# Two head pairs' k and v by the hardware queue in fp32, larger tile bursts, and a new order of pieces, in a fused linear-attention and channel-mix kernel

## The chip, the cores and the metric

One core of a Trainium2 chip runs the whole program. Its engines each work through their own list of instructions in order: TensorE (PE in the profile; PEld is its weight load), VectorE (DVE), ScalarE (ACT), GpSimd (POOL, which here only issues loads) and SyncE (SP, which here only issues transfers). They meet through semaphores. The metric is the device time of one execution in microseconds, median of several runs.

## The reference

What has to be computed, cut to its core (B = 8 batches, H = 8 heads, S = 576 positions, D = 64, so C = H * D = 512; F = 1024):

```python
kv  = einsum('bhsd,bhse->bhde', k, v)
o   = einsum('bhsd,bhde->bhse', q, kv)
o   = o / sqrt(mean(o * o, -1) + 1e-6) * g_norm
x   = o.transpose(0, 2, 1, 3).reshape(B, S, C)
x_prev = x shifted by one position, zeros first
xk  = mu_k * x + (1 - mu_k) * x_prev ;  xr likewise with mu_r
k2  = maximum(xk @ w_k, 0) ;  out = sigmoid(xr @ w_r) * ((k2 * k2) @ w_v)
```

All inputs and the output are fp32 in DRAM.

## The kernel before

The work is cut into named pieces. A piece is a Python function that records a few instructions on one engine; `plan.emit` (L60 on) goes through the string `ORDER` word by word and records the pieces in that order, so each engine's list of instructions is the order of its words. A word `name@D` or `name@A` says on which of VectorE and ScalarE a piece runs that could run on either. Nothing is reordered later: an engine whose next piece waits stands still, whatever is ready behind it.

Attention of batch b, in two halves z = 0, 1 of four heads each:

- `ld.q`, `ld.k`, `ld.v` (L251) load a tensor through GpSimd's software queue, which converts fp32 to bf16 on the way. Batches 0 and 1 load by z, 288 KB each as bf16; later batches load whole, 576 KB. The weights (`ld.wk0`, `ld.wk1`, `ld.wr`, `ld.wv0`, `ld.wv1`, L266, 512 KB each) use the same queue. At most eight of its transfers are under way: the ninth issue waits until the first has landed. Loads also wait until one of three buffers of their tensor is free.
- `kv` (L286) makes the 64 x 64 products of k and v, `q` (L294) transposes q, `u` (L301) multiplies the two. All three use quarters of TensorE's array (64 x 64 tiles); the rest of TensorE's work uses the whole array, except `ss` of batches 2 and up. Their results stand in two PSUM buffers, `at`. `kc`, `qc` and `uc` copy them to SBUF (L172 on ScalarE, L174 on VectorE), and `sq` squares u. `u`, `uc` and `sq` come in two column parts each: `u3.01` is batch 3, z = 0, part 1.
- `ss` sums squares per head. In batches 2 and up one `ss` serves all heads (L409), `rs` takes the reciprocal root (L306, tile `rsc`), and `sp.z` (L455), on SyncE, copies its rows to all partitions by four transfers for each z. `mul.z` (L423, VectorE) multiplies into `xT`.
- `wr.z` copies 63 columns inside `xT`, `d` subtracts neighbours, `mk` and `mr` scale the difference, `xk` and `xr` (L331) add: the inputs of the channel mix.

The channel mix, in nine groups g of 512 rows that straddle the batches: `k` (L518 for g = 0, L542) with `relu` (L503) and `ksq` (L552); `r` (L564) with `sig` (L574); `v` (L584) with `out` (L597), which multiplies by `sig`; `st` (L493), on SyncE, stores 128 rows by two transfers. `mm`, two PSUM buffers, holds the results of k, r and v in turn, and `out` has three SBUF buffers, each free again when both of its stores have landed. `g.wk`, `g.wr` scale the weights by g_norm. `z:512` (L482) is a matmul of zeros that adds nothing; it only keeps TensorE working.

Of the kernel before, what the change touches and what calls it, by code (L numbers as in the profile page):

```python
# [7 lines left out]
FP32 = mybir.dt.float32  # L8
# [7 lines left out]
ld.q0.0 seta small setb ld.k0.0 ld.v0.0 ld.q0.1 ld.v0.1 ld.k0.1 ident ld.wk0 id9 ld.q1.0 z:512 z:512 z:512 z:512  # L16
z:512 z:512 z:512 z:512 z:512 z:512 z:512 q0.01 ld.wk1 tr9 qc0.01@A cols z:512 q0.00 qc0.00@A ld.v1.1 z:512 z:512
z:512 z:512 z:512 z:512 z:512 z:512 kv0.0 ld.v1.0 kc0.0@A z:512 u0.01 u0.00 uc0.01@D uc0.00@A ld.k1.1 sq0.01@D
sq0.00@D z:512 z:512 z:512 z:512 z:512 ss0.01 ss0.00 rs0.01 ld.k1.0 rs0.00 mul0.01 z:512 z:512 q0.11 qc0.11@D ld.wr
mul0.00 z:512 kv0.1 q0.10 d0.0a kc0.1@A qc0.10@D mk0.0a@A z:512 u0.11 uc0.11@D u0.10 wr0.0@A sq0.10@A d0.0w sq0.11@D  # L20
uc0.10@A g.wk00@D ld.q1.1 z:512 z:512 z:512 z:512 ss0.10 xk0.0a d0.0b ss0.11 rs0.10 k0.000 ld.wv0 rs0.11 mul0.10
q1.0 g.wk01@A d0.1a mk0.1a@D mk0.0b@A xk0.1a mr0.0a@D table k0.001 g.wk10@D ld.wv1 g.wk11@D k0.010 mul0.11 relu0.00
d0.1b ld.q2.01 xk0.0b k0.011 mk0.0w@D mk0.1b@D k0.100 wr0.1@D relu0.01 xk0.1b ld.v2.01 d0.1w ksq0.00 k0.101 mr0.0b@A
mr0.1a@D k0.110 ld.k2.01 relu0.10 xr0.0b ksq0.01 mr0.1b@A xk0.0w ksq0.10 ld.v3.01 kv1 qc1.0@D kc1@A xr0.1b mr0.0w@A
xr0.0a u1.01 u1.00 uc1.01@A k0.111 uc1.00@A g.wr1@D ld.k3.01 g.wr0@D relu0.11 sq1.01@D r0.2 sq1.00@D ld.q3.01
# [5 lines left out]
sq2.00@A xr1.1 relu1.3 k1.5 ksq1.3 ss2 kv3 ksq1.1 rs2 q3.0 ld.k5.01 sp2.0 r1.0 kc3@A relu1.2 qc3.0@D r1.1 ksq1.0
u3.01 q3.1 uc3.01@D sp2.1 r1.2 ld.q6.01 sq3.01@D ld.v5.01 r1.3 sig1.0 qc3.1@D ld.v6.01 ksq1.2 u3.00 u3.10 v1.0.0
uc3.00@D uc3.10@A st0.0 sq3.10@A sq3.00@D v1.0.1 sig1.1 mul2.0 u3.11 q4.1 wr2.0@D d2.0 v1.1.0 mk2.0@A v1.1.1 mul2.1
v1.3.0 qc4.1@A out1.0 v1.2.0 wr2.1@A xk2.0 uc3.11@A st1.0 v1.2.1 sq3.11@A d2.1 v1.3.1 st0.3 mk2.1@D xk2.1 ss3 kv4
out1.1 q4.0 k2.2 ld.q7.01 qc4.0@D rs3 ld.v7.01 k2.3 kc4@D sp3.0 mr2.1@D u4.11 u4.00 uc4.11@D k2.4 uc4.00@A relu2.1
sq4.11@D k2.5 sq4.00@D sp3.1 mr2.0@D u4.01 relu2.2 u4.10 uc4.01@D k2.0 sq4.10@A sq4.01@D k2.1 ksq2.1 uc4.10@A st1.1
xr2.0 ss4 relu2.0 q5.1 xr2.1 k2.6 ksq2.0 k2.7 mul3.0 qc5.1@D r2.0 relu2.3 r2.1 wr3.0@A ksq2.3 rs4 r2.2 ksq2.2 sp4.0
d3.0 r2.3 sig2.0 mk3.0@D q6.1 mul3.1 kv5 sig2.1 q5.0 qc6.1@D st1.3 v2.3.0 kc5@A qc5.0@D v2.1.0 st0.2 wr3.1@D d3.1
u5.11 u5.01 sp4.1 uc5.11@A v2.2.0 mk3.1@D uc5.01@A xk3.1 v2.3.1 mr3.1@D v2.2.1 sq5.01@D st1.2 sq5.11@D v2.0.0 xk3.0
out2.1 u5.10 kv6 uc5.10@A q6.0 ld.k7.01 mul4.0 v2.0.1 st2.2 qc6.0@A mr3.0@D v2.1.1 kc6@A sq5.10@D st2.3 xr3.1 k3.2  # L40
out2.0 u6.10 u5.00 k3.3 uc5.00@A mul4.1 st2.0 k3.4 xr3.0 relu3.1 wr4.1@D k3.5 d4.1 uc6.10@A r3.0 mr4.1@D relu3.2
sq5.00@D r3.1 sq6.10@D wr4.0@D ksq3.1 u6.01 sig3.0 ss5 uc6.01@D k3.0 d4.0 k3.1 sq6.01@D mk4.1@D rs5 kv7 mr4.0@D
relu3.0 q7.0 sp5.1 xr4.0 u6.00 k3.6 kc7@A ksq3.2 qc7.0@A k3.7 mk4.0@D ksq3.0 r3.2 relu3.3 sp5.0 uc6.00@D r3.3
sq6.00@D xk4.0 u6.11 q7.1 uc6.11@D v3.1.0 st2.1 ksq3.3 v3.0.0 sig3.1 mul5.1 v3.1.1 qc7.1@A sq6.11@D xk4.1 ss6 xr4.1
v3.0.1 r4.0 out3.0 r4.1 rs6 st3.0 u7.10 u7.11 sq7.10@A v3.2.0 uc7.11@A st3.1 uc7.10@D v3.3.0 sq7.11@D wr5.1@D sp6.0
# [12 lines left out]
out7.1 r8.3 ksq8.2 st7.2 r8.0 sig8.1 r8.1 st7.3 v8.2.00 sig8.0 v8.2.10 v8.1.10 out8.20 v8.0.00 st8.20 out8.10
v8.0.10 st8.10 v8.3.01 out8.00 v8.3.11 v8.3.00 st8.00 out8.31 v8.3.10 st8.31 out8.30 st8.30
# [40 lines left out]
def kernel(  # L100
# [13 lines left out]
    nc = tc.nc  # L114
# [538 lines left out]
```

## Time and profile before

| | |
|---|---|
| Median of 3 runs | 209.78 us (208.43 to 209.99) |
| Span of the profiled execution | 206.6 us |
| TensorE busy | 193.2 us (94%), 2172 matmuls |
| VectorE busy | 137.8 us (67%) |
| ScalarE busy | 118.6 us (57%) |
| Software queue (q0) | 16.78 MB, 48.3% of 16 engines' span |
| Hardware queue of SyncE (q1) | 12.46 MB, 24.0% |
| v matmuls, L584 | 272 recorded, 62.6 us busy |
| k matmuls, L542 | 288 recorded, 59.2 us busy |
| r matmuls, L564 | 144 recorded, 34.1 us busy |
| Matmuls of zeros, L482 | 34, 10.9 us busy |

Busy times of TensorE overlap, since matmuls are pipelined: one of 512 columns lasts 379 ns, but in a run of them the next ends 216 ns later (16 in 3.45 us). So the place to read is where TensorE stood idle, and for what. The three parts of the span differ. Until about 39 us TensorE waits for the first batches; then it is busy almost without a gap until its last matmul at 202.8 us; 3.8 us remain for the last product and its store.

### The profile page before, as it was taken

The numbers are of one execution on the slowest core, as the hardware profiler recorded it, in microseconds if no ns is written. First come the engines' busy times: TensorE is split into PE (matmuls) and PEld (weight loads), VectorE is DVE, ScalarE is ACT, GpSimd is POOL, SyncE is SP. The second block draws the span as 40 slices with busy tenths as digits, with TensorE's granted clock in tenths as the row PEclk, the third lists the DMA queues.
The fourth block names the chain that finished last, engine by engine and source line by source line (L and its number), as shares of the span: only waits on it lengthen the run. The fifth ranks groups of instructions, "written<-read, shape, count | busy, mean of one in ns | idle before, by whom it ended". The sixth has DMA issues, their size and how long they took to land.

```text
span 206.6 us, 5133 instructions
## 1 busy us (share of the span) xinstructions
PE 193.2 (94%) x2172; PEld 95.7 (46%) x2172; DVE 137.8 (67%) x273; ACT 118.6 (57%) x151; POOL 26.4 (13%) x40
## 2 busy tenths in 40 slices
PE   7797979999799799799999999999999999999992
PEld 2344844544344444354443585444444444444441
DVE  1059988886585999698997798788733623421332
ACT  2279789867577395636896987716725032531310
POOL 7752532202140400000000000000000000000000
PEclk9999999999999999999999999999999999999999
DMA  4999999999999999999433650346004242604155
GB/s 75 162 207 205 206 208 205 208 216 221 210 238 236 231 252 242 223 264 268 116 91 77 149 122 0 71 94 156 0 0 102 62 93 61 143 0 102 24 133 153
DMA packets 25211, 30.10 MB, mean 146 GB/s; under 512 B 2524, under 2 KB 20708, under 8 KB 25188
## 3 DMA queue, kind: packets, MB, share of 16 engines
q0 software_dynamic: 15408, 16.78, 48.3%
q1 hardware_dynamic: 9380, 12.46, 24.0%
q10 hardware_dynamic: 400, 0.52, 0.7%
q8 instruction: 17, 0.28, 0.5%
q14 instruction: 6, 0.05, 0.1%
HBM read 33.56 MB, written 9.44 MB: 208 GB/s over the span
## 4 chain that ended last, share of the span: by engine, by line
PE 68%; DMA 20%; SPq 3%; ACT 2%; POOL 2%; issue 2%; DVE 1%; ACTq 0%; DVEq 0%; POOLq 0%
PE mm L584 26%; PE mm L542 24%; PE mm L564 12%; DMA w_r<-in_moe_w_r_dram 7%; DMA rs<-rsc 5%; DMA k<-in_k_dram 4%; DMA out_dram<-out 3%; SPq L455 2%; PE at L584 2%; PE at L301 2%; PE at L286 1%; PE at L294 1%; SPq L493 1%; POOL q L251 1%; ACT rsc L306 1%
## 5 line engine op out<-in xcount | busy, mean ns | idle before, releaser
L584 PE MATMUL mm<-w_v,sqk 128*128 128x512 bf16 x272 | 62.6, 379 | 0.0
L542 PE MATMUL mm<-xk,w_k 128*128 128x512 bf16 (+1 forms) x288 | 59.2, 356 | 0.0
L503 ACT ACTIVATE relu<-mm 128x1024 bf16<-128x1024 f32 x36 | 36.8, 1022 | 25.8 <-PE mm L542 23.4
L584 PEld LDWEIGHTS <-sqk 128*128 128x128 bf16 x296 | 28.2, 98 | 32.2 <-issue 1.4
L542 PEld LDWEIGHTS <-w_k 128*128 128x128 bf16 x288 | 27.2, 98 | 26.9 <-issue 1.6
L564 PE MATMUL mm<-w_r,xr 128*128 128x512 bf16 x144 | 34.1, 379 | 0.7 <-DVE w_r L180 0.7
L552 DVE TENSOR_TENSOR sqk<-relu 128x1024 bf16<-128x1024 bf16 x32 | 21.6, 687 | 16.4 <-ACT relu L503 16.4
L597 DVE TENSOR_TENSOR out<-mm,sig 128x1024 f32<-128x1024 f32 x16 | 19.6, 1222 | 18.6 <-PE mm L584 18.6
L574 ACT ACTIVATE sig<-mm 128x1024 bf16<-128x1024 f32 x18 | 18.3, 1024 | 22.5 <-PE mm L564 22.5
L564 PEld LDWEIGHTS <-xr 128*128 128x128 bf16 x144 | 13.7, 98 | 16.6 <-issue 1.0
L180 DVE TENSOR_SCALAR md<-d,cols 128x576 bf16<-128x576 bf16 (+2 forms) x62 | 18.2, 344 | 0.3
L172 ACT CAST uT<-at 128x576 bf16<-128x576 f32 (+1 forms) x18 | 11.4, 645 | 11.4 <-PE at L301 11.3
L423 DVE TENSOR_TENSOR xT<-uT,rs 128x1152 bf16<-128x1152 bf16 (+2 forms) x18 | 12.4, 686 | 4.8 <-DMA rs<-rsc 3.0
L188 ACT ACT_TABLE_LOAD x12 | 15.4, 1283 | 0.2
L174 DVE CAST uT<-at 128x576 bf16<-128x576 f32 (+1 forms) x14 | 10.4, 742 | 7.0 <-PE at L301 5.5
L318 DVE TENSOR_TENSOR d<-xT 128x1152 bf16<-128x1152 bf16 (+2 forms) x20 | 12.7, 634 | 0.8 <-ACT xT L172 0.5
L331 DVE TENSOR_TENSOR xk<-md,xT 128x1152 bf16<-128x1152 bf16 (+2 forms) x20 | 12.7, 633 | 0.6 <-ACT md L178 0.4
L331 DVE TENSOR_TENSOR xr<-md,xT 128x1152 bf16<-128x1152 bf16 (+2 forms) x20 | 12.5, 631 | 0.0
L482 PE MATMUL mm<-zero 128*128 128x512 bf16 x34 | 10.9, 452 | 1.2 <-DVE zero L209 1.2
L172 ACT COPY qT<-at 128x1152 bf16<-128x1152 bf16 (+2 forms) x8 | 8.0, 995 | 6.0 <-PE at L294 6.0
L178 ACT ACTIVATE md<-d,cols 128x256 bf16<-128x256 bf16 (+2 forms) x18 | 9.9, 600 | 1.8 <-DVE d L318 1.8
L174 DVE COPY qT<-at 128x1152 bf16<-128x1152 bf16 (+2 forms) x10 | 6.9, 693 | 4.7 <-ACT kv L172 4.2
(54 smaller groups left out, 139.3 us busy)
## 6 DMA issues: line engine op xcount, KB each, us to landing
out_dram<-out SPq DMA_DIRECT2D x67, 128.0 KB, 2.5
q<-in_q_dram POOLq DMA_DIRECT2D x6, 576.0 KB, 23.0
v<-in_v_dram POOLq DMA_DIRECT2D x6, 576.0 KB, 25.7
k<-in_k_dram POOLq DMA_DIRECT2D x6, 576.0 KB, 22.5
rs<-rsc SPq DMA_DIRECT2D x48, 72.0 KB, 5.0
q<-in_q_dram POOLq DMA_DIRECT2D x4, 288.0 KB, 9.7
k<-in_k_dram POOLq DMA_DIRECT2D x4, 288.0 KB, 11.4
v<-in_v_dram POOLq DMA_DIRECT2D x4, 288.0 KB, 11.0
```

The costliest lines, as they stand in the source:

```text
L172: nc.scalar.copy(out=dst, in_=src)
L174: nc.vector.tensor_copy(out=dst, in_=src)
L180: nc.vector.tensor_scalar(out=dst, in0=src, scalar1=col, scalar2=None, op0=ALU.mult)
L188: nc.scalar.preload_act_table_set(name)
L331: nc.vector.tensor_tensor(out=dst[:, 2 * z:2 * z + 2, r0:r0 + w], in0=md.t[:, :, cs], in1=xT[:, :, prev], op=ALU.add)
L503: nc.scalar.activation(out=get(rt), in_=ps.t, func=AF.Relu)
L542: nc.tensor.matmul(get(ps)[:, fc % 2, a0:a1], w_k_sb[:, cc, 128 * fc:128 * fc + 128], xk[:, cc, x0:x0 + a1 - a0], start=(cc == 0), stop=(c ...
L552: nc.vector.tensor_mul(out=get(sqk)[:, 2 * f2:2 * f2 + 2, :], in0=rt.t, in1=rt.t)
L564: nc.tensor.matmul(get(ps)[:, ci % 2, :], xr[:, cc, n0:n0 + 128], w_r_sb[:, cc, :], start=(cc == 0), stop=(cc == NHP - 1))
L574: nc.scalar.activation(out=get(sg), in_=ps.t, func=AF.Sigmoid)
L584: nc.tensor.matmul(get(ps)[:, bank, cs], sqk.t[:, fc, 128 * ci:128 * ci + 128], w_v_sb[:, fc, cs], start=(fc == 0), stop=(fc == NFC - 1))
L597: dv = add(f"out{g}.{c2}", "D", lambda _, ps=ps, sg=sg, ot=ot: nc.vector.tensor_mul(out=get(ot), in0=ps.t, in1=sg.t), deps=ms + [sg_done], ...
```

## The change

Four edits, and a new `ORDER` that carries them.

1. k and v of batch 0, z = 0 come by SyncE's hardware queue as fp32 (`hl.v0.0`, `hl.k0.0`), into one of the three buffers of their tensor, and are converted by two new copies of 128 x 1152 (`c.v0.0`, `c.k0.0`, both put on VectorE).
2. `kv` and both `q` of a batch become one piece, `kvq`; both column parts of a `u` become one piece (batches 1 and up).
3. Batch 1 has `kvq` by z, and the k pieces of group 1 take two column blocks and one z each, where they took one column block and all heads.
4. `ORDER` is new throughout. It has 22 matmuls of zeros where there were 34; `ld.wk1` is the first load of the software queue; the loads of batches 2 to 5 come batch after batch.

```diff
+    HW = ("k", "v")
...
+    def load_hw(b, n, z):
+        tmp, dst = Buf(n), kvq[(n, b)]
+        m = slice(2 * z, 2 * z + 2)
+
+        def fp32():
+            return get(tmp)[:, :, :].bitcast(FP32).rearrange("p (m a) c -> p m (a c)", m=2)
+
+        def fn(_):
+            view = src[n][b].rearrange("(m e) (p j) d -> (e p) m (j d)", e=2, j=NJ)
+            nc.sync.dma_start(out=fp32(), in_=view[:, m, :])
+
+        p = add(f"hl.{n}{b}.{z}", "S", fn, bufs=[tmp])
+        loaded[(n, b, z)] = add(f"c.{n}{b}.{z}", "DA", lambda eng: copy(eng, get(dst)[:, m, :], fp32()), deps=[p],
+                                bufs=[tmp, dst])
...
+                    if b == 0 and z == 0 and n in HW:
+                        load_hw(b, n, z)
+                    else:
+                        load(b, n, [z])
...
+                def burst(_, zs=zs, pss=pss):
+                    kv_tiles(get(pss[0]), KC, kin.t, vin.t, zs)
+                    for z, ps in zip(zs, pss):
+                        q_tiles(as_bf16(ps), qin.t, z, range(NJ))
...
+            def u_mm(_, i_s, z=z, qT=qT, uss=uss, parts=parts):
+                for i in i_s:
+                    u_tiles(get(uss[i]), kv.t, qT.t, z, *parts[i])
...
+                if g == 1:
+                    deps = (x_ready[0]["k"][2 * x:2 * x + 2] + [x_wrap["k"][x], x_ready[1]["k"][x]]
+                            + [p_wk[(f2 // 2, z)] for z in range(x + 1)] + [m])
+                    args = ([2 * f2, 2 * f2 + 1], [2 * x, 2 * x + 1])
```

The start of the new order, and its stretch from batch 2's `ss` to group 3's first k pieces (lines as they stand, cut at both ends):

```diff
+seta ident table setb hl.v0.0 c.v0.0@D small ld.wk1 ld.q0.0 ld.v0.1 id9 ld.q0.1 ld.k0.1 z:512 z:512 z:512 z:512 z:512
+z:512 z:512 z:512 z:512 z:512 z:512 z:512 z:512 z:512 tr9 hl.k0.0 c.k0.0@D kv0.0 cols kc0.0@D z:512 q0.01 g.wk10@A
+qc0.01@D q0.00 u0.01 qc0.00@A uc0.01@A sq0.01@D u0.00 sq0.00@A z:512 z:512 z:512 ss0.00 uc0.00@A rs0.00 mul0.00 ss0.01
...
+r1.2 ss2 relu1.0 rs2 st0.1 st0.0 sp2.1 ksq1.1 ksq1.2 ksq1.0 r1.0 r1.3 sig1.1 kvq3 r1.1 qc3.1@A qc3.0@D kc3@D mul2.1
+sp2.0 v1.1.0 u3.1 uc3.11@D sq3.11@A wr2.1@D uc3.10@A sq3.10@A v1.0.0 v1.0.1 v1.1.1 d2.1 mul2.0 sig1.0 u3.0 ld.v4.01
+ld.k4.01 ld.q4.01 wr2.0@A v1.2.0 v1.3.0 v1.3.1 out1.0 d2.0 mk2.1@D xk2.1 uc3.01@D sq3.01@A uc3.00@A sq3.00@A ss3 rs3
+v1.2.1 mk2.0@D xk2.0 kvq4 kc4@A qc4.0@A qc4.1@D out1.1 sp3.1 k2.2 k2.3 sp3.0 st1.2 st0.3 st0.2 u4.1 uc4.10@D mul3.1
+mr2.0@D relu2.1 sq4.11@A k2.0 k2.1 k2.6 uc4.11@A sq4.10@A wr3.1@A relu2.0 u4.0 k2.7 uc4.00@A k2.4 k2.5 ld.q5.01
+ld.v5.01 mr2.1@D relu2.3 xr2.1 xr2.0 ksq2.1 uc4.01@D mul3.0 wr3.0@D sq4.01@A sq4.00@A ld.k5.01 relu2.2 r2.2 ss4 rs4
+ksq2.0 sp4.0 sp4.1 st1.0 ksq2.3 r2.3 v2.3.0 sig2.1 ksq2.2 v2.3.1 v2.2.0 v2.2.1 out2.1 st2.3 st1.1 d3.0 d3.1 r2.0 r2.1
+st1.3 ld.v7.01 ld.q7.01 ld.v6.01 mk3.0@A ld.k6.01 ld.q6.01 ld.k7.01 sig2.0 v2.1.0 kvq5 qc5.1@A v2.0.0 v2.0.1 v2.1.1
+mk3.1@D mr3.1@D mul4.0 xk3.0 kc5@D qc5.0@A xk3.1 mul4.1 u5.0 k3.6 k3.7 out2.0 wr4.0@A xr3.1 wr4.1@D mr3.0@D xr3.0
+uc5.00@A uc5.01@A sq5.01@D sq5.00@D st2.2 relu3.3 d4.0 mr4.0@D ksq3.3 k3.0 k3.1 relu3.0 k3.4 u5.1 uc5.11@A k3.5 k3.2
```

More of the change, by code (lines that the diff above doesn't have):

```diff
@@ L15 @@
 ORDER = """
[L16 to L25, printed above, removed]
@@ L31 @@
[L31 to L40, printed above, removed]
@@ L41 @@
[L41 to L45, printed above, removed]
@@ L60 @@
+st8.30 st8.10 out8.00 st8.00 v8.3.01 v8.3.11 out8.31 st8.31
 """
@@ L260 @@
                 for z in range(NZ):
-                    load(b, n, [z])
+                    if b == 0 and z == 0 and n in HW:
+                        load_hw(b, n, z)
+                    else:
+                        load(b, n, [z])
             else:
@@ L368, in attention, with kv_copy @@
         qd, kvcs = {}, []
-        def kv_piece(name, ps, c, zs):
-            m = add("kv" + name, "T", lambda _: kv_tiles(get(ps), c, kin.t, vin.t, zs), bufs=[ps, kin, vin],
-                    deps=[loaded[(n, b, z)] for n in ("k", "v") for z in zs])
+        def kv_copy(name, dep, ps, c, zs):
             ks = slice(HD * zs[0], HD * zs[-1] + HD)
-            return m, add("kc" + name, "DA", lambda eng: copy(eng, get(kv)[:, :, ks], ps.t[:, :, c + ks.start:c + ks.stop]),
-                          deps=[m], bufs=[ps, kv])
@@ L385, in attention, with lds @@
+        def lds(ns, zs):
+            return [loaded[(n, b, z)] for n in ns for z in zs]
         if b == 0:
             for z in range(NZ):
-                _, kc = kv_piece(f"{b}.{z}", Buf("at"), 0, [z])
-                kvcs.append(kc)
+                ps = Buf("at")
+                m = add(f"kv{b}.{z}", "T", lambda _, ps=ps, z=z: kv_tiles(get(ps), 0, kin.t, vin.t, [z]),
+                        bufs=[ps, kin, vin], deps=lds("kv", [z]))
+                kvcs.append(kv_copy(f"{b}.{z}", m, ps, 0, [z]))
```

131 lines of the change are left out of this document (78 added, 53 removed).

## The prediction

> **What bounds it now.** First the page's slices:
>
> ```profile
> PE   7797979999799799799999999999999999999992
> PEclk9999999999999999999999999999999999999999
> DMA  4999999999999999999433650346004242604155
> ```
>
> TensorE has gaps in the first eight slices (39 us) and almost none after; loads fill the DMA engines until about 99 us. TensorE's timeline of the start:
>
> ```profile
> 1.19 4.56 PE L482 MATMUL mm<-zero 128*128 128x512 bf16 x11 [1.19 <-DVE zero L209]
> ...
> 7.31 1.90 PE L482 MATMUL mm<-zero 128*128 128x512 bf16 x8
> 9.95 0.48 PE L286 MATMUL at<-v,k 64*64 64x64 bf16 x36 [0.74 <-DMA v<-in_v_dram]
> ...
> 18.42 1.03 PE L518 MATMUL mm<-xk,w_k 128*128 128x256 bf16 x8
> 20.75 5.49 PE L518 MATMUL mm<-xk,w_k 128*128 128x256 bf16 x48 [0.89 <-DVE xk L331]
> ```
>
> Useful streaming starts at 18.42. Later idle time is short, and three waits hold most of it (windows of 4 us add up to 4.0 between 39 and 203):
>
> ```profile
> 54.39 0.48 PE L294 MATMUL at<-ident,q 64*64 64x64 bf16 x36 [1.20 <-DMA q<-in_q_dram]
> ...
> 68.42 0.83 PE L286 MATMUL at<-v,k 64*64 64x64 bf16 x72 [0.93 <-DMA k<-in_k_dram]
> ...
> 84.16 0.77 PE L286 MATMUL at<-v,k 64*64 64x64 bf16 x72 [1.42 <-ACT sig L574]
> ```
>
> The third is named after ScalarE, but its burst needed v of batch 5, which stands in the software queue behind tensors of batch 6; I count all three as load waits. Then the chain of waits between them:
>
> ```profile
> 52.13 0.39 PE at L409 x8
> ...
> 52.54 0.75 ACT rsc L306
> ...
> 53.31 0.66 SPq L455
> ...
> 58.14 6.66 DMA rs<-rsc
> ...
> 64.92 0.06 DVE xT L423
> ```
>
> From the end of `ss` (52.5) it takes until 64.9 to multiply the second half; the first was multiplied at 61.1 (VectorE's timeline). Eight spreads cost SyncE 5.4 us to issue, and each lands late. The tile view of `rsc` up to 100 us says
>
> ```profile
> DMA to landing us min/median/max: 5.0/6.7/7.0
> ```
>
> and after 100 us, when no load runs,
>
> ```profile
> DMA to landing us min/median/max: 2.0/2.1/2.7
> ```
>
> Stores show the same: median 6.5 until 90 us, 2.4 from 104 on. Whoever stands behind a spread's `mul` waits some 8.5 us from `ss`, or 12.3 for the second half.
>
> **Start.** Before, q landed first and `kv0.0` ran at 9.95. Now v goes out first on SyncE (0.75; its issue costs 0.6 if it is like a store's, more if rows count), then four small loads (0.37 + 3 x 0.25 = 1.1 us), then k, at about 3. No row shows such a load. Lower bound for k's landing: 3 + 2.2 (least row of a store with no loads running) + 1.4, which is what 288 KB take (GpSimd's issues, freed by landings, come at 8.68, 10.10, 11.56) = 6.6. Upper: 3 + 6.9 (worst store under load) + 2 x 1.4, sharing half and half = 12.7. I take 8.5: only about one load stands in the other queue then, so nearer the lower. Its cast on VectorE, which nothing covers: 0.75 (a copy of 1152 bf16 from PSUM) to 1.5 (two casts of 576 fp32, 0.752 each); I take 1.0. By the Trainium skill ("VectorE: DVE Perf Modes", the mode that uses both read ports) an fp32 copy inside SBUF makes two results a cycle, which would be the lower end; no run here shows it. So `kv0.0` at about 9.6 (7.4 to 14.2). `q0.01` needs q, now second in GpSimd's queue behind 512 KB of weights (2.6 us between landings): about 10. From there to the first k piece the old rows give about 8 (before: 8.5 from `kv0.0`), with the weight scaling, which the old start waited for, out of the way: 18.2 against 18.42, **-0.2** (bounds -2 to +4).
>
> Between there and the first burst of batch 2 (39.07) TensorE waited 0.89 + 0.28 + 0.60 + 0.66 = 2.4 us before. w_r is now the tenth transfer of the software queue rather than the fourteenth, which removes the 0.66; batch 1 by halves shortens the others, and the same products stay: **-1** (0 to -1.5). The fillers dropped here were in idle time and give nothing.
>
> **Bursts.** A switch between whole array and tiles costs about 0.1 us each way (a run of four lasts 0.97 on the chain behind a burst, 0.86 elsewhere). But the old order had already put pieces side by side: from batch 2 on it has 23 groups of tile work, the new one 24. Nothing, plus or minus 0.3. SyncE's one new load, the VectorE casts and table loads (12 switches in either) add nothing past the start.
>
> **Load waits.** Batch 5's v and k now precede everything of batches 6 and 7, and batches 3 and 4 are complete earlier. All three waits go: **-3.6** (0 at worst, if others take their place).
>
> **Spread waits.** This is where I expect the loss. The larger bursts need both `at` buffers back, and the copies that free them stand behind `mul` and `wr` on VectorE and ScalarE. Durations are from one start to the next in the old timelines: r, v and k pieces 0.86 (four matmuls) and 0.1 for a switch; `kvq` 0.74 + 0.73 as kv and q took; two parts of `u` 0.37; on VectorE `mul` 0.69 and a copy of 576 0.68; on ScalarE a copy or square 0.57, `wr` 0.25, `relu` 1.0. With t the end of an `ss`:
> - `u3.0`. TensorE between: r 1.83, `kvq3` 1.45, r and v 1.83, `u3.1` 0.47, three v 2.6, so at t + 8.2 it wants `u3.0`, whose second part needs `uc3.11`. That is behind `mul2.1` on VectorE: 8.5 + 0.69 + 0.68 = 9.9. Wait 1.6.
> - `ss3`. At 10.1 plus three v pieces 2.7 = 12.8 it wants `sq3.00`, fourth on ScalarE after `wr2.0`, which needs `mul2.0` (12.3 + 0.69): 13.0 + 0.25 + 3 x 0.57 = 15. Wait 2.2, taken as 1.8 with the wait of `kvq4` on the same copies.
> - `k2.4`. v 0.96, `kvq4` 1.45, two k 1.83, `u4.1`, three k, `u4.0`, one k 4.5: t + 8.8. It needs `relu2.0`, behind `wr3.1`, behind `mul3.1`: 8.5 + 0.69 + 0.25 + 1.0 = 10.4. Wait 1.6.
> - `v2.3`, behind squares that stand behind `mul3.0`: 0.7.
> - `k3.0`. It needs the PSUM that `out2.0` frees, and `out2.0` the buffer whose last store is `st1.1`. SyncE: root at t + 1.2, eight spreads 5.2, `st1.0`, `st2.3`, then `st1.1`'s second transfer at 9.6, landing 5.4 later at 15.0, and `out2.0` 1.2: 16.2. TensorE has 14.2 of work till then. Wait 2.0; 2.5 with the small ones behind.
>
> Sum **+8.2**. Lower bound +1, with every landing at 2.1; upper +11, at 6.7 throughout.
>
> **Sum.** -0.2 - 1 - 3.6 + 8.2 = +3.4. The profiled execution: TensorE's end moves from 202.8 to 206.2, the 3.8 us of tail stay (the last half product and its store are the same), span 210.0. The median lies 3.2 above the span; with the same distance, 213.2.
>
> **Rivals.**
> - *The spreads land in time.* Fewer transfers collide with them, and landings come at some 2 to 3 us while loads run. Then of +8.2 some 1 remains: -3.8, 206.0, faster. It decides below about 4 us from issue to landing: the loss has to fall to the 4.8 of the gains, and a straight line from 8.2 at 5.4 us to 1 at 2.1 is there at 3.8. Against it: 5.0 is the least of 24 rows, and the loads still run to nearly 100 us. 0.17.
> - *The waits overlap.* One slip gives later spreads time, so half of 8.2 stays: -0.7, 209.1. 0.20.
> - *k is held up at the start.* It waits behind the weights as stores do, lands at 12.7, and the first k piece is at 22: +4 more, 217. 0.13.
> - *TensorE's clock falls.* Fillers took 4.56/11 = 0.41 us at first, later 1.90/8 = 0.24, though PEclk shows 9 in both. The 14 first fillers end near 6.6 and the next matmul comes near 9.6, a pause of 3 us where before it was 0.74. If the slow pace returns, the tile work and the first k pieces of 9.6 to 19 lose about 2: 215.2. 0.08. The Trainium skill ("TensorE: Matmul & The Clock Gate", "What's actually happening") has just this: an idle window of about 3.4 us halves the clock. The slow first fillers agree; no run here shows a return.
> - *My forecast*, all terms near their values, 211.5 to 215: 0.42.
>
> **How the numbers follow.** Likeliest: 213.2. Faster by over 1% (below 207.7; about what a measurement can tell) is the first rival, 0.17; within 1% is the second, 0.20; slower is the rest, 0.63. For the range I leave out most of the first rival below and the far end of the late start above: 207.5 to 217.5.
>
> **What would show it.** Right: no wait on a q, k or v load past 40 us; `u3.0`, `ss3`, `k2.4` and `k3.0` idle 1 to 3 us each, released by VectorE or ScalarE, with idle time there behind `rs<-rsc`, and `out2.0` behind a store; spreads still at 5 us or more. Wrong: TensorE without such gaps between 55 and 100 us (then the first rival), or the first k piece far from 18.2. If TensorE's last matmul falls before 202, the sum failed in the spread term.

## The result and the profile after

The changed kernel takes 226.49 us (median of 4 runs, 225.53 to 226.83), the kernel before 209.88 in the same comparison: ratio 1.0806, 95% interval 1.0747 to 1.0866. That is slower, as forecast, but by 16.6 us where 3.4 were forecast, and outside the range of 207.5 to 217.5. The span of the profiled execution is 223.6 us (before: 206.6), TensorE's last matmul ends at 218.7 (202.8). Of the runs further down, e1, e8 and e12 had one execution each that was over 1.5% above their fastest, and the ratios leave it out while the medians hold it.

The page's slices of TensorE, its granted clock and the DMA engines, of the kernel after (5.6 us each):

```profile
PE   7176899999884993999899999999999999999991
PEclk9958999999997699699999999999999999999999
DMA  6999999999999979966502550550027704600274
```

Before, PEclk was 9 throughout. Now it drops in three places: slices 3 and 4, 13 and 14, and 17, each time in or behind a slice in which TensorE is mostly idle (slice 2 with the digit 1, slice 13 with 4, slice 16 with 3). The start first. VectorE's timeline has the cast of k:

```profile
11.45 0.95 DVE L173 CAST k<-k 128x1152 bf16<-128x1152 f32 x1 [6.17 <-DMA k<-in_k_dram]
```

SyncE issued that load at 2.60, so it was under way for 8.8 us; v, issued at 0.74 and alone until 3.5 us, when the software queue's first packets start, had landed at 4.4. TensorE's timeline (start, length, group, and in brackets the idle time ahead of it and what ended it):

```profile
12.45 0.70 PE L303 MATMUL at<-v,k 64*64 64x64 bf16 x36 [3.52 <-DVE k L173]
...
22.77 1.04 PE L559 MATMUL mm<-xk,w_k 128*128 128x256 bf16 x8
```

The first k piece comes 4.35 us later than before (18.42). This varies between executions: in e3, e4 and e6 below, which have the same start, k's cast begins at 9.97 to 10.29 and the first k piece comes at 21.57 to 22.30. The same timeline between 60 and 95 us:

```profile
68.82 0.32 PE L318 MATMUL at<-qT,kv 64*64 64x288 bf16 x4 [2.76 <-ACT sq L367]
...
70.82 5.28 PE L632 MATMUL mm<-w_v,sqk 128*128 128x512 bf16 x12 [0.46 <-ACT sig L622]
...
89.58 3.36 PE L584 MATMUL mm<-xk,w_k 128*128 128x512 bf16 x8 [3.98 <-ACT relu L544]
```

The three load waits at 54, 68 and 84 us are gone; `u3.0` and `k2.4` wait in their place, behind copies, as the forecast said. But look at the lengths too: twelve matmuls at 70.82 take 5.28 us, where twelve at full pace take 2.75. The chain of waits ahead of 89.58 leads back to a spread, and VectorE's multiply behind it:

```profile
81.19 6.20 DMA rs<-rsc
...
87.51 0.77 DVE xT L464
```

The windows view, in stretches of 3.4 us (stretch, its length, then busy us and instructions of TensorE, its weight load, VectorE, ScalarE and GpSimd, the granted clock, DMA share, GB/s):

```profile
65.90:69.30 3.40, 0.48 (x5) 0.22 (x5) 2.29 (x4) 1.18 (x3) 0.00 (x0) 1.00 1.20 230
69.30:72.70 3.40, 2.33 (x9) 0.94 (x9) 2.65 (x4) 1.65 (x4) 0.00 (x0) 0.51 1.21 208
...
86.20:89.60 3.40, 0.02 (x1) 0.02 (x1) 2.05 (x6) 1.30 (x3) 0.00 (x0) 1.00 1.19 246
89.60:93.00 3.40, 3.40 (x9) 1.21 (x9) 3.37 (x7) 2.16 (x4) 0.00 (x0) 0.53 1.15 274
```

A stretch in which TensorE hardly works (0.48, 0.02) is followed by one with a granted clock of 0.51 or 0.53. In the one at 89.6 it is busy all the time, with 9 matmuls; the same view has 22 in the next 3.4 us, at 0.96. Taken finer, the clock is halved from 11.3 to 18.15, from 69.35 to 76.2 and from 89.8 to 93.2 us, and full elsewhere until TensorE's work ends.

So the 15.9 us of TensorE's end are: +4.35 to the first k piece; -1.4 from there to the fourth v piece (42.0, before 39.07); and 176.7 us from there to the end where it was 163.7. Of these +13, idle time is +7.0 (10.9 against 4.0, from windows of 4 us). The remaining 6.0 are longer busy time; the halved clock at 69.35 to 76.2 and 89.8 to 93.2 accounts for about 4.6 of them, since TensorE is busy for 9.1 us there at half speed, and 1.4 stay unexplained.

### The profile page after: what moved, and what is told of

Its sections match the earlier page's. It is cut to its first block, busy times and chain, and to the rows that moved or that the text cites. A ratio compares the mean times of both kernels' runs of the same rounds, so it can differ in the third digit from the quotient of the medians.

```text
span 223.6 us, 5124 instructions
## 1 busy us (share of the span) xinstructions
PE 197.3 (88%) x2160; PEld 96.6 (43%) x2160; DVE 134.1 (60%) x260; ACT 130.0 (58%) x166; POOL 25.0 (11%) x38
## 3 DMA queue, kind: packets, MB, share of 16 engines
q1 hardware_dynamic: 9924, 13.64, 24.6%
## 4 chain that ended last, share of the span: by engine, by line
PE 49%; DMA 5%; DVE 5%; SPq 2%; ACT 2%; issue 1%; DVEq 0%; ACTq 0%
PE mm L584 17%; PE mm L632 17%; PE mm L612 10%; DMA rs<-rsc 4%; SPq L496 2%; DVE out L645 2%; PE at L632 2%; DMA out_dram<-out 1%; DVE d L335 1%; ACT relu L544 1%; PE at L318 1%; DVE sqk L600 1%; PE at L311 1%; DVE xT L464 1%; PE at L303 1%; SPq L534 1%
## 5 line engine op out<-in xcount | busy, mean ns | idle before, releaser
L632 PE MATMUL mm<-w_v,sqk 128*128 128x512 bf16 x272 | 64.5, 390 | 0.5 <-ACT sig L622 0.5
L584 PE MATMUL mm<-xk,w_k 128*128 128x512 bf16 (+1 forms) x288 | 60.4, 362 | 5.0 <-ACT relu L544 4.0
L632 PEld LDWEIGHTS <-sqk 128*128 128x128 bf16 x296 | 29.2, 100 | 35.3 <-issue 4.1
L645 DVE TENSOR_TENSOR out<-mm,sig 128x1024 f32<-128x1024 f32 x16 | 19.6, 1223 | 26.0 <-PE mm L632 11.3
L367 ACT ACTIVATE sq<-at 128x576 bf16<-128x576 f32 (+2 forms) x23 | 14.9, 660 | 15.6 <-DVE uT L173 14.3
L177 ACT ACTIVATE md<-d,cols 128x576 bf16<-128x576 bf16 (+2 forms) x26 | 17.0, 719 | 5.4 <-DVE d L335 5.4
L179 DVE TENSOR_SCALAR md<-d,cols 128x576 bf16<-128x576 bf16 (+2 forms) x54 | 15.0, 337 | 0.2
L173 DVE CAST uT<-at 128x576 bf16<-128x576 f32 (+1 forms) x17 | 12.6, 755 | 1.8 <-PE at L318 1.8
L348 DVE TENSOR_TENSOR xk<-md,xT 128x1152 bf16<-128x1152 bf16 (+2 forms) x20 | 12.6, 634 | 0.2
L318 PE MATMUL at<-qT,kv 64*64 64x288 bf16 (+2 forms) x128 | 8.2, 309 | 4.4 <-ACT sq L367 3.5
L173 DVE COPY qT<-at 128x1152 bf16<-128x1152 bf16 (+1 forms) x9 | 6.4, 716 | 7.1 <-PE at L311 6.9
L171 ACT COPY qT<-at 128x1152 bf16<-128x1152 bf16 (+2 forms) x9 | 8.6, 965 | 3.5 <-PE at L311 2.4
```

Source lines behind the costliest of these rows:

```text
L173: nc.vector.tensor_copy(out=dst, in_=src)
L177: nc.scalar.mul(out=dst, in_=src, mul=col)
L179: nc.vector.tensor_scalar(out=dst, in0=src, scalar1=col, scalar2=None, op0=ALU.mult)
L348: nc.vector.tensor_tensor(out=dst[:, 2 * z:2 * z + 2, r0:r0 + w], in0=md.t[:, :, cs], in1=xT[:, :, prev], op=ALU.add)
L584: nc.tensor.matmul(get(ps)[:, fc % 2, a0:a1], w_k_sb[:, cc, 128 * fc:128 * fc + 128], xk[:, cc, x0:x0 + a1 - a0], start=(cc == 0), stop=(c ...
L632: nc.tensor.matmul(get(ps)[:, bank, cs], sqk.t[:, fc, 128 * ci:128 * ci + 128], w_v_sb[:, fc, cs], start=(fc == 0), stop=(fc == NFC - 1))
```

## The experiments

Each run is compared with the kernel before on the same chip. Where a gain over the changed kernel is given in us, it is the difference of the two ratios times 209.6; with these intervals it is good to 1.5 to 2.1 us.

| Run | Median us | Ratio to before | 95% interval |
|---|---|---|---|
| the changed kernel | 226.49 | 1.0806 | 1.0747 to 1.0866 |
| e1_fill_start | 223.39 | 1.0618 | 1.0537 to 1.0700 |
| e2_loads_first | 224.68 | 1.0705 | 1.0667 to 1.0743 |
| e3_repeat | 224.13 | 1.0676 | 1.0621 to 1.0731 |
| e4_mul_behind | 218.06 | 1.0380 | 1.0331 to 1.0428 |
| e5_soft_start | 224.67 | 1.0741 | 1.0688 to 1.0794 |
| e6_no_late_loads | 218.62 | 1.0439 | 1.0390 to 1.0488 |
| e7_start_order | 221.63 | 1.0587 | 1.0546 to 1.0629 |
| e8_searched | 214.41 | 1.0232 | 1.0170 to 1.0294 |
| e9_before_loads | 208.94 | 0.9973 | 0.9940 to 1.0006 |
| e10_before_searched | 207.83 | 0.9931 | 0.9903 to 0.9959 |
| e11_searched_again | 215.42 | 1.0279 | 1.0217 to 1.0342 |
| e12_refill_shift | 212.43 | 1.0114 | 1.0045 to 1.0183 |
| e13_small_bursts | 205.91 | 0.9823 | 0.9778 to 0.9868 |

### The clock at the start: e1_fill_start

```diff
 z:512 z:512
+z:512 z:512 z:512 z:512 z:512 z:512 z:512 z:512 z:512 z:512 z:512
 tr9 hl.k0.0 c.k0.0@D
+z:512 z:512 z:512 z:512 z:512 z:512 z:512 z:512 z:512 z:512 z:512 z:512 z:512 z:512
 kv0.0 cols
```

> The changed kernel with 11 more fillers ahead of tr9 and 14 more ahead of kv0.0, so that TensorE has work from 6.0 to about 12 us, where it was idle but for tr9; nothing else is moved. Theory A (the halved granted clock from 11.3 to 18.2 us is set by that pause, and it costs time): the granted clock stays at 1.0 through the start, the first k piece comes at 21.3 rather than 22.8, and the time falls by 1 to 2 us. Rival (the start goes at the pace of the landings and of the copies, and the slow clock hides behind them): the clock stays up as well, but the first k piece stays at 22.3 to 22.8 and the time within 0.5 us.

Measured: faster by 3.9 us. The windows view of this run, where the changed kernel has a clock of 0.50 in the same stretch:

```profile
11.30:14.70 3.40, 2.65 (x86) 1.48 (x85) 0.89 (x4) 2.05 (x3) 1.95 (x3) 1.00 1.21 206
```

The first k piece comes at 21.36, 1.4 us earlier. The times alone would not settle it, because e3, e4 and e6, which have the changed kernel's start and its halved clock, reach it at 21.57 to 22.30. But `kv0.0` runs at the same time here and in the changed kernel (12.50 and 12.45), and from it to the first k piece it takes 8.86 us here and 10.32 there, with 10.8 to 11.2 in those three. So the halved clock costs about 1.5 us at the start, as theory A has it. The fillers give a part of it back: k's cast is done at 11.40, and `kv0.0` stands behind them for 1.1 us.

The gain is larger than the 1 to 2 expected. In the profiled execution 2 us more come from later waits: those ahead of `u3.0` and `k2.4` are gone, one of 3.22 stands at `ss3`, and one that no semaphore ended stands behind `kvq3`:

```profile
62.94 0.82 PE L633 MATMUL mm<-w_v,sqk 128*128 128x512 bf16 x3 [2.02 <-issue]
```

Such pauses come up again in e11. What is shown is that the pause from 6.0 to 12.45 sets the clock and that the clock costs time at the start; the rest of the 3.9 us is not taken apart.

### The order of the transfers at the start: e2_loads_first

```diff
+ld.q0.0
 seta ident table setb hl.v0.0
+hl.k0.0
 c.v0.0@D small ld.wk1
-ld.q0.0
 ld.v0.1 id9 ld.q0.1 ld.k0.1
...
-tr9 hl.k0.0
 c.k0.0@D kv0.0
+tr9
...
-g.wk10@A
...
 ss0.01 rs0.01
+g.wk10@A
```

> The changed kernel with the start's transfers in another order: k on SyncE's queue right behind v, ahead of the four small loads; q as the first of the software queue, ahead of the 512 KB of w_k; tr9 behind kv0.0 and the scaling g.wk10 behind rs0.01, so that neither holds up the first products. Theory A (the late start is a matter of order: k stood behind small loads, q behind weights): k lands at 7 to 9 rather than 11.4, q at 7 to 8 rather than 12.6, the first k piece comes at 17 to 19 rather than 22.8, and the time falls by 4 to 6 us. Rival (a transfer of the hardware queue starves beside the software queue whatever its place): k still lands at 10.5 or later, the first k piece stays past 21, and the gain is below 1.5 us.

Measured: faster by 2.1 us. k's cast now starts at 6.11 us and `kv0.0` at 6.93, so the landings are as theory A says and the rival is out. But the first k piece came only at 20.2, not at 17 to 19. TensorE's timeline shows what came late next:

```profile
14.33 0.48 PE L311 MATMUL at<-ident,q 64*64 64x64 bf16 x20 [2.59 <-DMA q<-in_q_dram]
```

That is q of the second half, now behind the 512 KB of w_k. With that wait TensorE fell to half clock, from 14.3 to 24.6 us.

### The clock in the middle: e3_repeat

```diff
+            if word.startswith("rep:"):
+                self.pieces[word[4:]].fn("T")
+                continue
...
+rep:v1.0.0 rep:v1.0.1 rep:v1.1.0 rep:v1.1.1
 u3.0
...
+rep:k2.6 rep:k2.7 rep:k2.6 rep:k2.7
 k2.4
```

> The changed kernel with four pieces computed over again into the same PSUM ahead of u3.0 (v1.0 and v1.1, 16 matmuls) and four ahead of k2.4 (k2.6 and k2.7 twice, 16 matmuls): 3.5 us of work at full clock in each of the two long waits of 2.8 and 4.0 us, and no wait is taken away. Theory A (the two pauses also halve the clock for the next 3.4 to 6.8 us, which costs about 4.4 us): the granted clock stays near 1.0 at 69 to 76 and at 89 to 93 us, the twelve matmuls behind u3.0 take 2.6 rather than 5.3 us, and the time falls by 3 to 4 us although there is more work. Rival (the loss there is the waits alone): the time rises by 0.3 to 1 us.

Measured: faster by 2.7 us (1.0 to 4.4), although TensorE does 32 matmuls more. The clock is full from 66 to 74.8 us and from 89 to 93, and the twelve matmuls behind `u3.0` take 2.75 us. But the time won there met a wait that had been shorter:

```profile
75.44 0.67 PE L454 MATMUL at<-sq,heads 128*32 128x288 bf16 x8 [3.02 <-ACT sq L371]
```

`ss3` waited 0.49 in the changed kernel and 3.02 here, and with it the clock fell again, from 74.8 to 81.7:

```profile
72.85:76.26 3.41, 0.81 (x9) 0.27 (x9) 2.03 (x5) 2.58 (x4) 0.00 (x0) 0.79 1.21 206
76.26:79.67 3.41, 3.41 (x140) 2.11 (x142) 0.00 (x0) 1.27 (x3) 0.32 (x1) 0.50 0.42 81
79.67:83.09 3.42, 3.20 (x44) 1.36 (x34) 2.02 (x3) 1.68 (x3) 2.65 (x4) 0.71 0.77 126
```

By the medians the rival, a time that rises, is out. The twelve matmuls (2.75 against 5.28 us) show what the clock costs on the spot. That this reaches the end is not shown: in the profiled executions it takes 162.2 us from `ss2` to TensorE's last matmul here and 161.8 in the changed kernel, so the time won was given back at `ss3`. The clock costs less than its windows suggest where the next wait is for something that does not move.

### The order around the spreads: e4_mul_behind

```diff
-qc3.1@A qc3.0@D kc3@D mul2.1
-wr2.1@D
-d2.1 mul2.0
 uc3.01@D sq3.01@A uc3.00@A sq3.00@A
+mul2.1 wr2.1@D d2.1 mk2.1@D xk2.1 mul2.0
 ss3 rs3
+wr2.0@A d2.0
...
 sq4.01@A sq4.00@A
+mul3.1 wr3.1@A
...
+st1.0 st1.1 st1.3
 sp4.0 sp4.1
...
 sig2.1
+mul3.0 wr3.0@D
```

> The changed kernel with TensorE's order untouched: mul2 and mul3 of batches 2 and 3 with the wrap copies behind them are moved behind the copies and squares that free TensorE's buffers (uc3, sq3, uc4, sq4, relu2), and three stores go ahead of the spreads of batch 4. Theory A (the new waits of TensorE between 64 and 110 us are copies that stand behind a product which waits for its spread, and the slow clock follows from them): the waits ahead of u3.0, ss3, k2.4 and of the k piece at 108.9 go, one of some 3 us ahead of k2.2 comes in their place, and the time falls by 8 to 11 us, to 215.5 to 218.5. Rival (the spreads land so late that the blended tokens bind by themselves, whatever stands behind them): the waits move to the k pieces of groups 2 and 3 with nearly their whole length, and the gain is below 3 us.

Measured: faster by 8.9 us, theory A; from `ss2` to the last matmul it takes 154.5 us instead of 161.8, so the gain is in the middle. The waits at `u3.0`, `k2.4` and at the k piece of 108.87 are gone, 1.00 stays at `ss3`, and the one that was to come in their place is there, 2.1 us long:

```profile
75.74 2.88 PE L584 MATMUL mm<-xk,w_k 128*128 128x512 bf16 x7 [2.13 <-DVE xk L348]
```

The clock is not mended with it: one halved window follows this wait (76.5 to 79.9), and at the start, which is the changed kernel's own, the clock is halved from 8.2 to 25.3 in this execution.

### The loads by SyncE undone: e5_soft_start

```diff
-    HW = ("k", "v")
+    HW = ()
...
+ld.q0.0
 seta ident table setb small
+ld.k0.0 ld.v0.0 ld.q0.1 ld.v0.1 ld.k0.1 ld.wk1
 id9
...
 qc0.11@A
+g.wk10@A
```

> The changed kernel with its two SyncE transfers undone: k and v of the first four heads by the software queue and without a cast, the start's loads in the order of the kernel before (q, k, v of the first half, then of the second, then w_k), and the scaling g.wk10 behind qc0.11, so that ScalarE does not stand behind w_k. Everything past the start is the changed kernel's. Theory A (the start costs the changed kernel its 4.4 us because k came at 11.4 and q at 12.6, and those 4.4 us reach the end): kv0.0 at 9.8 to 10.3 us, no halved clock before 20 us, first k piece at 18 to 19, time lower by 3 to 5 us. Rival (later waits on spreads and loads, which follow the pace of the transfers, take most of it back): first k piece at 18 to 19 too, but a gain below 1.5 us.

Measured: 1.4 us faster by the ratios, which the intervals do not tell from nothing; `kv0.0` at 9.56, the first k piece at 20.32 instead of 18 to 19. It waits 0.42 for the scaling of w_k, and the clock, which theory A had full before 20 us, is halved from 11.4 to 18.2 behind a wait of 3.23 ahead of `kv0.0`. Neither theory holds as written: the transfers alone are not the whole 4.4 us, and this run does not decide how much of the start reaches the end. e7 does.

### Without the late loads: e6_no_late_loads

```diff
-    kvq = {(n, b): Buf(n) for n in src for b in range(B)}
+    kvq = {(n, b): Buf(n) for n in src for b in range(4)}
+    kvq.update({(n, b): kvq[(n, 1 + (b - 1) % 3)] for n in src for b in range(4, B)})
...
         def fn(_):
+            if b >= 4:
+                return
```

> The changed kernel without the loads of q, k and v for batches 4 to 7: these batches read the buffers of batches 1 to 3 again (that part of the output is not the reference's; the work of every engine is otherwise the same). The software queue is empty from about 60 us on, where it runs to about 95 us otherwise. Theory A (spreads and stores land late because the loads fill the 16 DMA engines): the multiply of the first spread comes 2 to 3.5 us after its last issue rather than 6.3, the waits ahead of u3.0, ss3 and k2.4 fall below 1 us each, and with them the halved clock at 69 to 76 and 89 to 93 us goes; time lower by 8 to 12 us. Rival (a spread is slow by itself, from its issue of 0.65 us each and its small rows): the multiply still comes 5 us or more after the last issue, the three waits keep more than half their length, and the gain is below 3 us.

Measured: faster by 7.7 us. The tile view of `rsc`, from 50 to 100 us:

```profile
DMA to landing us min/median/max: 2.0/2.1/3.2
```

In the kernel before it is 5.0/6.7/7.0 in the same stretch; the changed kernel's own view gives no such line, and the landing on its chain took 6.20. The waits ahead of `k2.4` and at the first part of `u3.0` are gone, and the clock is full from 20.5 us until TensorE's work ends. So late landings are made by the loads: theory A. One number missed: `ss3` still waits 3.02 us, for a square behind the copy `uc3.01` at 70.33, and that copy stands on VectorE behind `mul2.0`, `out1.0`, `d2.0` and `xk2.1`. There the order binds, not the landing.

### The start alone: e7_start_order

```diff
+ld.q0.0
 seta ident table setb hl.v0.0
+hl.k0.0
 c.v0.0@D small
-ld.wk1 ld.q0.0
+ld.q0.1
 ld.v0.1 id9
-ld.q0.1
 ld.k0.1
+ld.wk1
...
-tr9 hl.k0.0
 c.k0.0@D
+z:512 z:512 z:512 z:512 z:512 z:512
 kv0.0
+tr9
...
-g.wk10@A
...
 qc0.11@A
+g.wk10@A
```

> The start alone once more, after the run with k behind v and w_k second, in which k landed at 6.1 us but the second half's q came at 14.3: k right behind v on SyncE, the software queue in the order q, q, v, k and only then w_k, the scaling g.wk10 behind qc0.11, tr9 behind kv0.0, six more fillers ahead of kv0.0. Theory A (the start is a matter of the order of its transfers, and its gain reaches the end): kv0.0 near 7.5, q of the second half before 10, no TensorE wait above 1.5 us and no halved clock, first k piece at 17 to 18.5, time lower by 4 to 6 us. Rival (what is won at the start is given back at the spreads of batches 2 to 4, since the loads run at the same pace to 95 us whatever the start): first k piece at 17 to 18.5, but a gain below 2.5 us and longer waits between 60 and 110 us.

Measured: faster by 4.6 us. `kv0.0` runs at 7.21, no wait of the first 19 us behind the first filler is over 1.0 us, the clock is full until 65.9, and the first k piece comes at 17.09, 5.7 us earlier than in the changed kernel. `ss2` is 4.6 us earlier (52.31 against 56.87), and TensorE's last matmul 4.2: theory A. The waits of the middle are together as long as in the changed kernel (1.95, 1.59 and 3.93 at `u3.0`, `ss3` and `k2.4`, there 2.76, 0.49 and 3.98), so almost nothing is given back there.

### Both parts, and what is left: e8_searched, e11_searched_again, e12_refill_shift

e8 has the first loads of e7 in their order and a new order of the pieces up to group 7, in which `mul2.1` and its kin follow the copies; e11 is the same once more with later landings counted in. The stretch from `ss2` on in e11:

```diff
+ss2 r1.2 ksq1.2 r1.3 rs2 kvq3 qc3.0@D kc3@D relu1.0 sig1.1 r1.0 ksq1.0 qc3.1@A u3.1 r1.1 ld.q5.01 sp2.1 sq3.10@A
+ksq1.1 uc3.11@D sq3.11@A v1.1.0 uc3.10@A u3.0 uc3.01@D sp2.0 mul2.1 ld.k5.01 v1.1.1 wr2.1@D sig1.0 d2.1 v1.0.0
+v1.0.1 mk2.1@D uc3.00@A sq3.01@A sq3.00@A v1.2.0 ss3 v1.3.0 rs3 out1.0 ld.v5.01 kvq4
```

> Both parts together, with the order of the pieces from the first burst to group 7 found anew: that start order, and every product that waits for a spread placed behind the copies and squares that free TensorE's buffers. The same pieces, the same instructions. Theory A (start, spread waits and the clock that falls in them are the whole loss, and the larger bursts and the missing load waits are worth the 4 us that were counted for them): no TensorE wait above 1.5 us past 40 us, no halved clock past 25 us, time 203 to 208, faster than the kernel before. Rival (the loads and spreads bind by themselves with this loading): 209 or more.

> The changed kernel with both parts mended once more, as in the run with start and mid order found anew, this time with the landings of spreads taken at 6 to 8 us, as the trace of that run shows them, and w_k at 15.7. Theory A (what was left there were two waits of 2.2 and 2.1 us and a halved clock at 19 to 22 us, all three of them from landings that were taken too early): no wait above 1.5 us past 40 us, time 207 to 211. Rival (the waits move on to the next product that needs a spread): 213 to 215 again.

Both miss: 12.0 and 11.0 us faster than the changed kernel, but 214.4 and 215.4 instead of 203 to 208 and 207 to 211. A part of the start is lost again: the first k piece comes at 20.66 (e8) and 19.48 (e11), where e7 had 17.09, and the clock is halved from 18.5 to 21.9 and from 16.4 to 23.3. Waits for spreads are down to 2.22 (e8) and to none above 0.7 (e11). What is there instead is this, in e11, inside the burst of batch 5:

```profile
88.18 0.32 PE L311 MATMUL at<-ident,q 64*64 64x64 bf16 x7 [3.16 <-issue]
```

"issue" means that no semaphore released it: seven transposes of a burst stand 3.16 us behind the others of the same piece, which waits for nothing in its middle. e8 has the same at 88.67 (2.08). The DMA view of 85 to 88.5 us of e11 has a queue that the view of the eleven us before has not:

```profile
q8 instruction: 1, 0.02, 1.7%
```

It is one packet of 16 KB; the page counts 17 of them (0.28 MB), and its 4320 matmuls and weight loads make about 254 for each. A burst with its weight loads is 288 instructions in 1.4 us. And the pause is followed by half clock:

```profile
88.20:91.60 3.40, 3.40 (x15) 1.36 (x15) 0.00 (x0) 3.06 (x5) 0.00 (x0) 0.51 1.20 243
```

By the Trainium skill ("Runtime: NRT & Kernel Launch", "Instruction fetch mechanics") instructions stream in blocks of 16 KiB, 256 instructions, and the cost of a block's end is mostly hidden. The size agrees with the trace; hidden it was not, 3.16 us. If TensorE waits here for its instructions, it matters where a burst lies between two blocks, and e12 moves it by 44 instructions:

```diff
+z:16 z:16 z:16 z:16 z:16 z:16 z:16 z:16 z:16 z:16 z:16
+z:16 z:16 z:16 z:16 z:16 z:16 z:16 z:16 z:16 z:16 z:16
 ss0.10
```

> The second searched version of the changed kernel with 22 tiny fillers (16 columns each) ahead of ss0.10, where TensorE waits 2.4 us anyway: 44 more TensorE instructions, 1 to 1.5 us of work inside that wait, so that every later burst stands 44 instructions further on in TensorE's stream. Theory A (the stall of 3.16 us in the middle of the burst of batch 5, which no semaphore explains, is TensorE waiting for its own instructions: a packet of 16 KB, 256 instructions, of the instruction queue starts at 85.8 us, and the burst eats 256 instructions in 1.3 us; whether a burst stalls depends on where it stands between two such packets): the stall at batch 5 shrinks to 1 us or less, the time falls by 2 to 3.5 us. Rival (the stall is a wait that the profile does not name, on a load or a buffer of batch 5): it stays at 2.5 us or more in the same place, the time is within 1 us.

Measured: 212.43, faster than e11 by 1.65% of the time before, 3.5 us, with twenty-two matmuls more. The same burst:

```profile
86.09 0.42 PE L312 MATMUL at<-ident,q 64*64 64x64 bf16 x29 [0.68 <-issue]
```

Theory A: the pause shrinks in its place, and the time falls by what was said. But the 3.5 us are a net figure, since the same shift brought a new pause of 2.46 us of this kind at 62.09, between `kvq3` and an r piece; that was not foreseen.

The other traces bear the cause out. Past 25 us they hold eight pauses of over 0.5 us that no semaphore ended: one each in e1, e7, e8 and e13, two each in e11 and e12. Each ends 2.2 to 2.4 us after a 16 KB packet of this queue starts. And the number of matmuls and weight loads ahead of it, divided by 256, leaves a rest of 165 to 180 every time: the pauses stand at one place of the block.

### The parts on the kernel before: e9_before_loads, e10_before_searched, e13_small_bursts

e9 moves loads only (the words of the loads alone are shown):

```diff
-ld.k6.01
 ld.q4.01 ld.v4.01 ld.k4.01 ld.q5.01 ld.k5.01
+ld.v5.01
 ld.q6.01
-ld.v5.01
+ld.k6.01
 ld.v6.01
```

> The kernel before with one part of the change alone: the order of the loads of batches 3 to 6 in the software queue (q, v, k of batch 4 ahead of k of batch 6, k and v of batch 5 ahead of q and k of batch 6). Nothing else is moved. Theory A (load waits and spread waits overlap: a burst that comes earlier meets copies that still stand behind a spread): two or all three of the load waits of 1.20, 0.93 and 1.42 us go, waits of 1 to 2 us released by ScalarE or VectorE come at ss3 and k2.2 in their place, and the time falls by less than 1 us. Rival (the step of the prediction: the three load waits are worth 3.6 us by themselves): the time falls by 2.5 to 3.6 us.

Measured: ratio 0.9973, no difference that can be told. All three load waits are gone, and this came:

```profile
67.53 0.30 PE L408 MATMUL at<-sq,heads 128*32 128x288 bf16 x2 [1.02 <-ACT sq L354]
```

with 0.55 and 0.68 close behind it. Theory A: the load waits were worth at most 1.3 us, not 3.6.

e10 is the kernel before with its order found anew from the first products to group 7; its stretch behind `ss2` starts so:

```diff
-ss2 kv3 ksq1.1 rs2 q3.0 ld.k5.01 sp2.0 r1.0 kc3@A relu1.2 qc3.0@D r1.1 ksq1.0 u3.01 q3.1 uc3.01@D sp2.1
+ss2 rs2 k1.7 k1.4 k1.5 uc2.00@D relu1.3 kv3 xr1.1 q3.1 ld.q6.01 ksq1.0 q3.0 kc3@A st0.1 qc3.0@D ld.q5.01
```

> The kernel before with its own small bursts, its own loads and its own start, but the order of the pieces from the first product to group 7 found anew with the late landings of spreads and stores counted in: products that wait for a spread behind the copies that free TensorE's buffers, stores where they hold no spread, loads in the order of need. Theory A (the order around spreads and loads is what costs; the size of the bursts and the loads by SyncE are worth nothing by themselves): no wait of TensorE above 1 us past 35 us, time 205 to 208. Rival (the old order was as good as its landings allow): within 1 us of the kernel before, or slower.

Measured: 207.83, 0.7% faster than before (0.4 to 1.0%), inside theory A's range, if near its end; no wait above 0.6 us past 35 us. The half of theory A that puts the bursts and the SyncE loads at nothing is not decided by this run. Its start gave back a part: a load wait of 1.44 us at 27.85.

e13 adds the two SyncE loads to that, in the order of e7, with fillers:

```diff
+ld.q0.0 seta ident setb hl.v0.0 hl.k0.0 c.v0.0@D small ld.q0.1 ld.v0.1 ld.k0.1 id9 ld.wk0 ld.q1.0
...
+tr9 c.k0.0@D cols kv0.0 q0.00 kc0.0@A q0.01 ld.wk1
```

> The other combination: the small bursts of the kernel before in its searched order, with the changed kernel's loads of the first k and v by SyncE (k right behind v, q and the second half ahead of w_k in the software queue) and fillers where TensorE waits between 10 and 17 us. Theory A (the two transfers by SyncE are worth 1 to 2 us at the start once their order is right, and small bursts do not outrun TensorE's instruction fetch): first k piece at 17 to 18.5, no wait above 1.2 us past 30 us, no wait without a releaser, time 205 to 207.5, faster than both kernels. Rival (the start is bound by the copies between products, not by the loads): first k piece at 19.5 or later and 207.5 to 209.

Measured: 205.91, 1.8% faster than the kernel before (1.3 to 2.2%), the fastest of all versions, and 1.1% ahead of e10. The first k piece comes at 17.12. The page's slices of TensorE:

```profile
PE   7776999999999998999999999999999999999992
```

The one 8 past the start is a pause without a releaser, in a small burst too, so that part of theory A is wrong as it was written:

```profile
81.91 0.32 PE L305 MATMUL at<-v,k 64*64 64x64 bf16 x15 [1.16 <-issue]
```

## Why the prediction was wrong

The direction was right, and its reason too: copies behind products that wait for a spread. The size was wrong by 13 us. In the profiled executions TensorE's end moved by 15.9 us where 3.4 were forecast: the start is 4.6 us of that difference, idle time in the middle 2.4 and longer busy time there 6.0, less 0.4 between start and middle. By its own steps:

- **Start, -0.2: measured +4.35** (3.2 to 3.9 in e3, e4 and e6, with the same start). This term failed. k landed at 11.4, within the bounds of 6.6 to 12.7 but far from the 8.5 taken, q at 12.6 where "about 10" was said. "Only about one load stands in the other queue then" was the wrong reason: w_k and q, 800 KB, were issued ahead of k at 1.52 and 2.40, six more loads followed by 6.7 us, and they shared the engines with k. e2 and e7 show that the order makes the difference (k lands at 6.1 us, and in e7 the first k piece comes at 17.09). The cast was sized right: 0.95 against 1.0. v's, with the same shape, took 0.76, and so did k's in e1 to e4 and e6; in e7, e11 and e13 it took 0.92 to 1.12, and no run shows why. By the Trainium skill ("VectorE: DVE Perf Modes", the mode that uses both read ports), as the prediction cites it, it would be at the lower end, 0.75; the trace agrees for v.
- **From there to the first burst of batch 2, -1: measured -1.4.** Right.
- **Bursts, 0 ± 0.3.** Nothing in the changed kernel's own trace speaks against it: it has no pause without a releaser above 0.2 us. But the price of a burst of 288 instructions was not asked at all, and e1, e8, e11 and e12 show pauses of 2.0, 2.1, 3.2 and 2.5 us in or behind one. So the changed kernel's order was lucky in its one profiled execution: e1, which only adds fillers at its start, has one.
- **Load waits, -3.6.** All three went, but e9 shows that removing them alone is worth at most 1.3 us. The step counted each wait by its length, and did not ask what the burst meets when it comes earlier.
- **Spread waits, +8.2.** The mechanism is shown by e4 (8.9 us back by order alone) and e6 (7.7 by faster landings). Idle time in the middle rose by 7.0, where 8.2 less 3.6 had been forecast. By place: `u3.0` 2.76 (forecast 1.6), `k2.4` 3.98 (1.6), `ss3` and its neighbours 1.7 (1.8), the piece that waits for `out2.0` 0.86 (2.0 to 2.5), `v2.3` none (0.7).
- **"TensorE's clock falls", a rival at 0.08 and 2 us, at the start alone.** It happened three times, and the forecast's own sum has nothing for it. At the start it costs about 1.5 us between `kv0.0` and the first k piece (e1), near the 2 that the rival gave. In the middle it accounts for about 4.6 of the 6.0 us of longer busy time; that these would be won without it is not shown, since e3 gave back at `ss3` what it won. The prediction saw pauses of 1.6 to 2.5 us coming and did not put the rule to them that it had cited. By the Trainium skill ("TensorE: Matmul & The Clock Gate", "What's actually happening") an idle window of 3.4 us halves the clock; here pauses of 2.76 and 3.98 us were enough, with 0.44 and 0.25 us of work in the 3.41 us up to the fall at 69.35 and 89.83. Nor is a halved clock always lost time: the three other runs of the changed kernel have a mean granted clock of 0.936 to 0.946 where the profiled one has 0.960, by an estimate from clock and span 6 to 11 us more at half clock, and their spans are only 0.7 to 1.3 us longer.

The steps that failed are the start's term, mis-sized by 4.6 us, and the clock, put at nothing in the sum and tied to the start alone. The rivals were also taken as exclusive: "k is held up" (+4) and "the clock falls" (+2) were alternatives to the forecast, each with its own time, while all of them came at once. The forecast with both added is 219, already outside the range.

What stays open: e12 and e13 differ by 6.5 us, in burst size, in the pieces of batch 1 and in order. The pauses without a releaser (2.46 + 0.68 in e12, 1.16 in e13) can be a part of it; the rest was not taken apart. Nor was it tried whether the changed kernel's runs outside the profiled one have such pauses.

## What to carry to other kernels

A pause of TensorE of 2 us or more is to be priced with the half-speed stretch that can follow it, and waits that can come together are to be added, not weighed against each other. Place a product that waits for a transfer behind every copy that frees a buffer for the busiest engine, and order the transfers of a start by the first use of each, whichever queue they take. A wait that is removed is worth only the distance to the next one on the same path, and the other waits in the trace show that distance.

## What the runs showed of the hardware

- The halved clock comes in windows that run by themselves. Its three stretches in the changed kernel last 6.83, 6.83 and 3.41 us, and their beginnings, 11.32, 69.35 and 89.83, are 17 and 6 times 3.41 us apart. In the traces of the changed kernel and of e1 to e13, TensorE was busy for less than 1.25 us in 17 of these windows at full clock, and half clock followed all of them; with 1.3 to 2.2 us it followed some, above that none. A wait of 2.13 us was enough in e4, where 1.23 us of work stood in the window; the pause of 2.46 us in e12 did nothing, with 1.37 us of work in the emptiest window that it touched. Full clock came back only after a window with 2.8 us of work or more.
- Under a full software queue, a small transfer of SyncE takes 5.0 to 7.0 us from issue to landing, with the queue empty 2.0 to 3.2 (e6). A load of 576 KB in fp32 took 3.7 us alone, and beside that queue 8.8 in the changed kernel and 7.4 to 8.0 in e1, e3, e4 and e6.
- TensorE can outrun its own instructions: where work goes on only 2.2 to 2.4 us after a 16 KB packet starts, that is too late for a burst that uses 256 instructions in 1.3 us. It shows as idle time with "issue" as its releaser, inside a piece or right behind one.
